# Norms of a layer's output tiles: sums taken with the residual's addition and squares on ScalarE, in place of statistics instructions

## The chip, the cores and the metric

The kernel runs on one core of one Trainium2 chip. Its engines are TensorE (PE for the products, PEld for loading their weights), VectorE (DVE), ScalarE (ACT), GpSimd (POOL) and SyncE (SP, which issues the transfers). Each engine has a queue of its own that it works through in order; an instruction that waits holds back all that stand behind it on that engine. The metric is the device time of one execution in microseconds.

## The reference

Four layers on x of 2048 rows by 640 columns, each `x = x + layer(layernorm(x))`: sliding-window attention, a Fourier mixing, attention again, Fourier mixing again.

```python
def _layernorm(x, axis=-1, eps=1e-5):
    m = jnp.mean(x, axis=axis, keepdims=True)
    v = jnp.var(x, axis=axis, keepdims=True)
    return (x - m) / jnp.sqrt(v + eps)
...
    x = A_x
    x = x + _A_ref(_layernorm(x, axis=-1), A_wqkv, A_wo)
    x = x + _B_ref(_layernorm(x, axis=-1), B_dft_seq_re, B_dft_seq_im, B_dft_hid_re, B_dft_hid_im)
    x = x + _A_ref(_layernorm(x, axis=-1), A_wqkv, A_wo)
    x = x + _B_ref(_layernorm(x, axis=-1), B_dft_seq_re, B_dft_seq_im, B_dft_hid_re, B_dft_hid_im)
    return x
```

`_A_ref` has 32 heads of width 20 with a window of 256, and ends in a product with `wo` (640 by 640). `_B_ref` is the real part of a Fourier transform over the hidden and the sequence dimension, written as products with matrices of cosines and sines.

## The kernel before

All large products are made in three parts: each operand is cut into a rounded piece (hi) and the rest (lo), and hi·hi + hi·lo + lo·hi is summed in PSUM. The cut is `split` (line 157): ACT writes hi (line 160), then DVE or, where `eng` says so, POOL subtracts to get lo (line 166).

The rows are worked on in 16 tiles of 128 (NB = 16). An attention layer ends in `after_heads`. By then the heads are done, and for each tile the product of the heads' outputs with the first three of five chunks of `wo` has been added to the residual; the sum lies in `y_part(t)`. What is left for each tile is in `late` (line 925): the product with the last two chunks (12 matrix products of 128x320, two halves in two PSUM banks in turn), the addition of each half to y into a tile xw (line 970; line 964 is the same for a tile made while heads still run), the store of xw, and the norm of xw, which the next layer needs.

The norm before takes `bn_stats` twice (line 218), `bn_aggr` (220), an addition of eps (222), a sign change of the mean (976), all on DVE; then the power -1/2 on POOL (`root`, line 981); then on ACT a one-column product (934) and the scaling of the whole tile (931), whose result goes back into `y_part(t)`. The next layer's first products use tiles in pairs j and j + 8. For t below 8, `split_x` cuts columns 0 to 384 of the normed tile (hi on ACT, lo on POOL). For t from 8 on, POOL first adds columns 384 to 640 of the pair's two tiles (`sum1`, line 1047), and `split_x` then cuts that sum. Tiles 14 and 15 (`fast`) go another way: DVE norms the columns that are needed first.

Between the tiles PE works on units of the Fourier layer (`unit`, `seq`; units 0 to 7 are "a1", unit 8 + j is "a2" of pair j): each multiplies one cut slice of a normed tile by one cut piece of the transform matrix, 9 products of 128x512. `cut_to` cuts these pieces one or two units ahead (the hi on ACT, sums and lo on DVE, line 166 with c or qp). When `let_go` is called, operations held back for the heads' outputs are written out (line 782, line 166 with kp).

The order of all this is written out once, by a planner in the program that counts time. `post(d, f)` writes f's instructions d ticks later; `tick` goes one tick on; `spend(us)` adds planned time and ticks once per 0.65 us (PACE). One step of a tile's product spends 0.147, a unit 2.05. A unit is written only when the tiles that it needs are normed and cut (`normed` against `need`); `after_heads` writes a tile, then one unit (two after tile 4), and so on. The posts of tile t, counted from the end of its additions: power +2; scaling +5; for t below 8 the cut +2 after that, for the others sum1 +1 and the cut +3 after that; the store of xw +5. `sum3` (line 1051, POOL) follows at +4 for t from 7 on.

The copies of line 1323 take finished sums of units 0 to 7 out of PSUM on ACT, posted +1, +4 and +7 after unit 7. ACT runs copies, scalings and, in the heads, exponentials.

Of the kernel before, what the change touches and what calls it, by code (L numbers as in the profile page):

```python
# [7 lines left out]
F32 = mybir.dt.float32  # L8
# [3 lines left out]
AF = mybir.ActivationFunctionType  # L12
OP = mybir.AluOpType
# [4 lines left out]
P = 128  # L18
S = 2048
D = 640  # L20
# [5 lines left out]
NB = S // P  # L26
# [3 lines left out]
EPS = 1e-5  # L30
# [33 lines left out]
class Net:  # L64
# [860 lines left out]
    def late(self, xsrc, xdst, hook):  # L925
        nc = self.nc
        ks = range(EARLY, KC)
        w = dict(zip(ks, self.late_w))

        def scaled(t, xw, st, nm, c0, c1):  # L930
            nc.scalar.activation(self.y_part(t)[:, c0:c1], xw[:, c0:c1], AF.Identity, bias=nm[:, 1:2], scale=st[1][:, 1:2])  # L931

        def norm(t, xw, st, nm):
            nc.scalar.activation(nm[:, 1:2], nm[:, 0:1], AF.Copy, scale=st[1][:, 1:2])
            scaled(t, xw, st, nm, 0, D)
            if t < NB // 2:
                self.post(2, lambda: self.split_x(t, 0, 384))
            else:
                j = t - NB // 2
                self.post(1, lambda: self.sum1(j, nc.gpsimd))  # L940
                self.post(3, lambda: self.split_x(j, 384, 640))

        def norm_last(t, xw, st):

            xn, j = self.y_part(t), t - NB // 2
            nc.vector.tensor_scalar(out=xn[:, 384:], in0=xw[:, 384:], scalar1=st[0][:, 0:1], scalar2=st[1][:, 1:2],
                                    op0=OP.subtract, op1=OP.mult)
            self.sum1(j, nc.vector)
            self.post(1, lambda: self.split_x(j, 384, 640, nc.vector))

        def norm_rest(t, xw, st, nm):
            nc.scalar.activation(nm[:, 1:2], nm[:, 0:1], AF.Copy, scale=st[1][:, 1:2])
            scaled(t, xw, st, nm, 0, 384)

        for t in range(NB):
            sb, i = t // 4, t % 4
            y = self.y_part(t)
            xw = self.raw()
            both = [slice(hf * 320, (hf + 1) * 320) for hf in range(2)]
            if not self.after:  # L960
                ps = [self.bank("w", 320) for _ in both]
                yield from self.in_turn(ps, [self.out_terms(self.late_o[sb], w, ks, i, hf) for hf in range(2)])
                for p, cs in zip(ps, both):
                    nc.vector.tensor_tensor(out=xw[:, cs], in0=p, in1=y[:, cs], op=OP.add)
            else:
                for hf, cs in enumerate(both):
                    p = self.bank("o", 320)
                    for _ in self.product3(p, self.out_terms(self.late_o[sb], w, ks, i, hf)):
                        yield 1
                    nc.vector.tensor_tensor(out=xw[:, cs], in0=p, in1=y[:, cs], op=OP.add)  # L970
                    if hf == 0:
                        yield 1
            self.post(5, lambda t=t, xw=xw: nc.sync.dma_start(xdst[t * P:(t + 1) * P, :], xw))
            st = self.stats(xw, False)
            nm = self.ln.tile([P, 2], F32, name="nb", tag="nb")
            nc.vector.tensor_scalar_mul(nm[:, 0:1], st[0][:, 0:1], -1.0)
            self.let_go()
            fast = t >= NB - 2

            def root(st=st):  # L980
                nc.gpsimd.tensor_tensor(out=st[1][:, 1:2], in0=st[1][:, 0:1], in1=self.half, op=OP.pow)  # L981
            if fast:
                root()
            else:
                self.post(2, root)
            if NB // 2 - 1 <= t < NB - 1:
                self.post(4, lambda t=t: self.sum3(t - NB // 2 + 1))
            if fast:
                d = 3 if t == NB - 2 else 0
                self.post(4 + d, lambda t=t, xw=xw, st=st: norm_last(t, xw, st))  # L990
                self.post(8 + d, lambda t=t, xw=xw, st=st, nm=nm: norm_rest(t, xw, st, nm))
            else:
                self.post(5, lambda t=t, xw=xw, st=st, nm=nm: norm(t, xw, st, nm))
            if t == NB - 2:
                u = self.last_a2 - 1
                self.post(3, lambda u=u: self.staged(u, 0, nc.vector))
                self.post(6, lambda u=u: self.staged(u, 1))
                self.post(9, lambda u=u: self.staged(u, 2))
            hook(t)
            self.late_t = t + 1  # L1000
            yield 0
# [728 lines left out]
```

## Time and profile before

| | us |
|---|---|
| median of 3 runs | 2174.63 (2174.54 to 2177.93) |
| the profiled execution, its own time | 2173.64 |
| its span from first to last instruction | 2171.9 |
| PE / DVE / ACT / POOL busy | 2116.4 / 1611.6 / 1167.9 / 932.6 |

The granted TensorE clock was 0.997 in the mean. A line of a profile names the source line, the engine, the operation, out<-in with their shapes and the count, then the busy time and the mean of one in ns, and after the second bar the engine's idle time just before such instructions, with what ended it. The chain of waits follows the work back from the last instruction, at each step to what released it, and lists the pieces in order of time: start, length, engine, tile, line. A table by stretches gives for each stretch the busy time of every engine, the granted clock, the share of the DMA engines and their GB/s. Rows of `big` hold the tiles y and their cut slices, `x` the tiles xw, `nb` the column that holds minus the mean, `rs` the one that holds the variance and its power, `c`, `qp`, `rr` cut pieces of the transform matrix.

The norms of the output tiles are made twice, at the end of layer 1 and of layer 3: 14 tiles the common way and two the fast way in each.

### The profile page before, as it was taken

What the parts mean: (1) busy time and instruction counts of PE and PEld (TensorE: products, weight loads), DVE (VectorE), ACT (ScalarE), POOL (GpSimd) and SP (SyncE); (2) the same over time, 40 slices, a digit from 0 to 9 for tenths busy, and PEclk for the clock granted to TensorE, in tenths of its full rate; (3) what the DMA queues carried; (4) which work ended last, traced back from release to release, by engine and by line L of the source; (5) the groups of instructions that cost most, each with busy time, mean ns of one, the idle gap of its engine ahead of it and who ended that gap; (6) DMA issues with size and microseconds to landing.
All of it is one profiled execution on the core that took longest, in us unless ns stands there. A gap on an engine that the chain in (4) does not pass through costs nothing.

```text
span 2171.9 us, 49261 instructions
## 1 busy us (share of the span) xinstructions
PE 2116.4 (97%) x17893; PEld 1768.5 (81%) x17893; DVE 1611.6 (74%) x3933; ACT 1167.9 (54%) x2611; POOL 932.6 (43%) x1458
## 2 busy tenths in 40 slices
PE   7999999899999999999999999998999999999999
PEld 7987777687878888889999877776777788888899
DVE  6348888786897968787751578887768878688777
ACT  3117887766554545543431288786665545455522
POOL 3037777876514224230230477777754333242300
PEclk9999999999999999999999999999999999999999
DMA  5546666786435353657646466667853454546653
GB/s 184 177 146 198 203 190 212 218 233 200 135 122 180 132 187 126 224 196 258 214 140 189 152 201 187 207 193 224 233 184 130 130 189 136 165 148 218 221 176 125
DMA packets 221619, 395.41 MB, mean 182 GB/s; under 512 B 39360, under 2 KB 85952, under 8 KB 221376
## 3 DMA queue, kind: packets, MB, share of 16 engines
q1 hardware_dynamic: 221376, 392.26, 57.0%
q8 instruction: 141, 2.31, 0.5%
q14 instruction: 102, 0.84, 0.1%
HBM read 273.94 MB, written 117.05 MB: 180 GB/s over the span
## 4 chain that ended last, share of the span: by engine, by line
PE 81%; DVE 6%; POOL 4%; ACT 4%; DMA 3%; issue 2%; SPq 0%; ACTq 0%; POOLq 0%; DVEq 0%
PE banks L1269 27%; PE banks L173 14%; PE banks L191 13%; PE banks L613 8%; PE banks L1524 6%; PE banks L583 6%; PE banks L553 4%; POOL ou L1199 1%; POOL big L166 1%; DVE qp L166 1%; ACT big L931 1%; PE banks L273 1%; PE banks L565 1%; POOL rs L981 1%; ACT big L160 1%
## 5 line engine op out<-in xcount | busy, mean ns | idle before, releaser
L558 DVE CUSTOM_DVE_ANT_0 banks<-banks,mask 128x384 f32<-128x384 f32 (+2 forms) x1024 | 525.5, 559 | 153.4 <-PE banks L553 117.5
L592 ACT ACTIVATE pt<-banks 128x384 f32<-128x384 f32 (+2 forms) x1024 | 430.1, 472 | 139.8 <-PE banks L553 59.5
L583 PE MATMUL banks<-qp,kp 61*128 61x384 f32 (+2 forms) x1024 | 302.8, 365 | 9.7 <-DMA qp<-mt 7.7
L598 POOL TENSOR_SCALAR_AFFINE_SELECT pt<-pt 128x256 f32<-128x256 f32 x512 | 213.5, 418 | 174.9 <-ACT pt L592 128.4
L553 PE MATMUL banks<-kp,qp 60*128 60x384 f32 (+2 forms) x1024 | 279.1, 359 | 4.8 <-DVE mc L558 4.5
L191 PE MATMUL banks<-big,wc 64*128 64x512 f32 x1920 | 272.1, 394 | 0.4 <-DVE pt L374 0.4
L583 PEld LDWEIGHTS banks<-qp,kp 61*128 61x128 f32 x1024 | 176.8, 185 | 68.0 <-issue 27.4
L613 PE MATMUL banks<-pt,vq 128*32 128x128 f32 x5760 | 215.3, 277 | 4.4 <-POOL pt L598 4.4
L191 PEld LDWEIGHTS banks<-big,wc 64*128 64x128 f32 x1920 | 183.3, 185 | 29.1 <-ACT x L477 6.7
L613 PEld LDWEIGHTS banks<-pt,vq 128*32 128x32 f32 x5760 | 144.3, 109 | 65.2 <-issue 48.2
L1199 POOL TENSOR_TENSOR pt<-pt,pt 128x512 f32<-128x512 f32 x36 | 62.8, 1744 | 293.0 <-DMA pt<-c 188.3
L602 POOL TENSOR_SCALAR_AFFINE_SELECT pt<-pt 128x256 f32<-128x256 f32 x448 | 187.4, 418 | 0.0
L553 PEld LDWEIGHTS banks<-kp,qp 60*128 60x128 f32 x1024 | 163.7, 185 | 26.7 <-DVE mc L558 16.3
L160 ACT ACTIVATE c<-pt 128x512 fp32r<-128x512 f32 x150 | 93.5, 626 | 151.0 <-POOL pt L1175 52.4
L160 ACT ACTIVATE qp<-pt 128x512 fp32r<-128x512 f32 (+1 forms) x195 | 119.9, 624 | 92.2 <-DVE pt L1200 38.9
L166 DVE TENSOR_TENSOR c<-pt,c 128x512 fp32r<-128x512 f32 x150 | 125.0, 843 | 52.0 <-ACT c L160 49.8
L166 DVE TENSOR_TENSOR qp<-pt,qp 128x512 fp32r<-128x512 f32 (+1 forms) x195 | 150.2, 783 | 12.4 <-ACT qp L160 9.8
L1269 PE MATMUL banks<-qp,big 128*128 128x512 f32 x630 | 151.2, 391 | 4.9 <-DVE qp L166 3.9
L558 DVE DVE_READ_ACCUMULATOR2_ANT mc<- 128x1 f32 x1024 | 145.2, 142 | 0.0
L1269 PEld LDWEIGHTS banks<-qp,big 128*128 128x128 f32 x630 | 117.0, 188 | 31.0 <-DVE qp L166 5.6
L1269 PE MATMUL banks<-qp,xc 128*128 128x512 f32 x480 | 117.9, 390 | 1.5 <-DVE xc L166 1.2
L1269 PEld LDWEIGHTS banks<-qp,xc 128*128 128x128 f32 x480 | 89.8, 188 | 21.9 <-DVE xc L166 2.1
(224 smaller groups left out, 4388.6 us busy)
## 6 DMA issues: line engine op xcount, KB each, us to landing
pt<-c SPq DMA_DIRECT2D x188, 512.0 KB
qk_d<-c SPq DMA_DIRECT2D x80, 512.0 KB
kp<-qk_d SPq DMA_DIRECT2D x384, 80.0 KB
qp<-qk_d SPq DMA_DIRECT2D x384, 80.0 KB
kp<-u_d SPq DMA_DIRECT2D x32, 640.0 KB
o_d<-ou SPq DMA_DIRECT2D x64, 256.0 KB
x_d<-x SPq DMA_DIRECT2D x48, 320.0 KB
v_d<-pt SPq DMA_DIRECT2D x16, 768.0 KB
```

What stands on the lines that cost most here:

```text
L160: nc.scalar.activation(hi, src, AF.Copy, scale=-1.0 if neg else 1.0)
L166: (eng or nc.vector).tensor_tensor(out=lo, in0=src, in1=hi.bitcast(F32), op=OP.subtract)
L173: self.nc.tensor.matmul(p, x, y, start=n == 0, stop=n == last)
L191: self.nc.tensor.matmul(ps[a], x[r], y[r], start=half + i == 0, stop=half == 1 and i == n - 1, skip_group_check=True)
L553: nc.tensor.matmul(p, qp[quad % 2][b:b + 60, z, qb * P:(qb + 1) * P], kp[quad % 2][b:b + 60, z, k0 * P:(qb + 1) * P], start=True, stop=True)
L558: nc.vector.tensor_tensor_reduce(out=p, in0=p, in1=self.mask[:, 384 - n * P:], scale=1.0, scalar=NEG, op0=OP.add, op1=OP.max, accum_out=mc ...
L583: nc.tensor.matmul(self.banks[:, tb[e], :n * P], kp[quad % 2][b:b + 61, z, kb * P:(kb + 1) * P], qp[quad % 2][b:b + 61, z, kb * P:(kb + n) ...
L592: nc.scalar.activation(pt[quad, kb][:, 2 * z + e, :n * P], self.banks[:, tb[e], :n * P], AF.Exp, scale=SCALE)
L598: nc.gpsimd.affine_select(out=t[:, :, 0:P], in_=t[:, :, 0:P], pattern=[[0, 2], [1, P]], compare_op=OP.is_ge, fill=0.0, base=0, channel_mul ...
L602: nc.gpsimd.affine_select(out=t[:, :, 256:384], in_=t[:, :, 256:384], pattern=[[0, 2], [-1, P]], compare_op=OP.is_gt, fill=0.0, base=0, ch ...
L613: nc.tensor.matmul(p[32 * h:32 * h + 32, :], vq[:, 96 * (kb % 4) + 21 * h:96 * (kb % 4) + 21 * h + 32], t[:, h, (qb - kb) * P:(qb - kb + 1 ...
L1269: nc.tensor.matmul(self.banks[:, bk, :], p, b[q], start=start and m == 0, stop=stop and last and m == 2, skip_group_check=True)
```

## The change

For tiles 0 to 13, the additions of line 970 become additions that also give each row's sum (`tensor_tensor_reduce`, the instruction that the heads use at line 558 with a maximum), into a new small tile `sa`. One DVE operation makes minus the mean of the two sums. The square of xw minus the mean is written by ACT (into y, where it is overwritten later by the scaling) with its row sum, one DVE operation makes the variance plus eps from it, and the power follows on POOL as before. `bn_stats`, `bn_aggr`, the addition of eps and the sign change go, for these tiles. The posts become: square +1, variance +3, power +4 (was +2), scaling +6 (was +5); what hangs on the scaling moves with it. Tiles 14 and 15 keep the instructions that they had.

```diff
+            fast = t >= NB - 2
+            sa = None if fast else self.ln.tile([P, 3], F32, name="sa", tag="sa")
+
+            def add(p, hf, y=y, xw=xw, sa=sa):
+                cs = both[hf]
+                if sa is None:
+                    nc.vector.tensor_tensor(out=xw[:, cs], in0=p, in1=y[:, cs], op=OP.add)
+                else:
+                    nc.vector.tensor_tensor_reduce(
+                        out=xw[:, cs], in0=p, in1=y[:, cs], scale=1.0, scalar=0.0,
+                        op0=OP.add, op1=OP.add, accum_out=sa[:, hf:hf + 1])
...
-                    nc.vector.tensor_tensor(out=xw[:, cs], in0=p, in1=y[:, cs], op=OP.add)
+                    add(p, hf)
...
-            st = self.stats(xw, False)
             nm = self.ln.tile([P, 2], F32, name="nb", tag="nb")
-            nc.vector.tensor_scalar_mul(nm[:, 0:1], st[0][:, 0:1], -1.0)
+            if fast:
+                st = self.stats(xw, False)
+                nc.vector.tensor_scalar_mul(nm[:, 0:1], st[0][:, 0:1], -1.0)
+            else:
+                st = None, self.ln.tile([P, 2], F32, name="rs", tag="rs")
+                nc.vector.tensor_scalar(out=nm[:, 0:1], in0=sa[:, 0:1], scalar1=sa[:, 1:2], scalar2=-1.0 / D,
+                                        op0=OP.add, op1=OP.mult)
             self.let_go()
-            fast = t >= NB - 2
...
+            def square(xw=xw, y=y, nm=nm, sa=sa):
+                nc.scalar.activation(y, xw, AF.Square, bias=nm[:, 0:1], scale=1.0, accum_out=sa[:, 2:3])
+
+            def variance(st=st, sa=sa):
+                nc.vector.tensor_scalar(out=st[1][:, 0:1], in0=sa[:, 2:3], scalar1=1.0 / D, scalar2=EPS,
+                                        op0=OP.mult, op1=OP.add)
             if fast:
                 root()
             else:
-                self.post(2, root)
+                self.post(1, square)
+                self.post(3, variance)
+                self.post(4, root)
...
             else:
-                self.post(5, lambda t=t, xw=xw, st=st, nm=nm: norm(t, xw, st, nm))
+                self.post(6, lambda t=t, xw=xw, st=st, nm=nm: norm(t, xw, st, nm))
```

More of the change, by code (lines that the diff above doesn't have):

```diff
@@ L962, in late @@
                 yield from self.in_turn(ps, [self.out_terms(self.late_o[sb], w, ks, i, hf) for hf in range(2)])
-                for p, cs in zip(ps, both):
-                    nc.vector.tensor_tensor(out=xw[:, cs], in0=p, in1=y[:, cs], op=OP.add)
+                for hf, p in enumerate(ps):
+                    add(p, hf)
             else:
@@ L969, in late @@
                         yield 1
-                    nc.vector.tensor_tensor(out=xw[:, cs], in0=p, in1=y[:, cs], op=OP.add)
+                    add(p, hf)
                     if hf == 0:
```

## The prediction

> **What bounds the kernel now.** I read the page's first part and chain of waits, then the stage that the change touches, by its line 970 (durations shortest/median/longest, then first and last start).
>
> ```profile
> span 2171.9 us, 49261 instructions
> PE 2116.4 (97%) x17893; PEld 1768.5 (81%) x17893; DVE 1611.6 (74%) x3933; ACT 1167.9 (54%) x2611; POOL 932.6 (43%) x1458
> PE 81%; DVE 6%; POOL 4%; ACT 4%; DMA 3%; issue 2%; SPq 0%; ACTq 0%; POOLq 0%; DVEq 0%
> ```
>
> ```profile
> L970 DVE TENSOR_TENSOR x<-banks,big x64: 473/478/492, 525.6 to 1666.0; 128x320 f32<-128x320 f32 x64
> ```
>
> TensorE sets the end of the whole, so only what moves TensorE counts. The table by stretches (columns: length, then busy us of PE, PEld, DVE, ACT, POOL) shows the stage of layer 1 in two parts and the second part of layer 3:
>
> ```profile
> 525.00:545.00 20.00, 16.58 (x92) 14.03 (x92) 19.23 (x49) 11.58 (x21) 8.48 (x10) 1.00 0.69 227
> 545.00:592.62 47.62, 44.62 (x235) 38.43 (x233) 40.23 (x104) 25.21 (x50) 27.07 (x34) 1.00 0.44 145
> 1625.00:1672.36 47.36, 44.32 (x234) 38.16 (x232) 39.96 (x104) 25.20 (x50) 27.07 (x34) 1.00 0.45 146
> ```
>
> The two layers agree, so I work out one stage and double it. PE is idle 3.42 + 3.00 = 6.4 us per stage: that is all that the change could win there. DVE is full in the first 20 us (19.23); ACT and POOL look half empty. They are not free, though. The chain of waits through the stage, in order of time (start, length, what):
>
> ```profile
> 548.07 0.93 ACT big L931
> ...
> 557.94 0.93 ACT big L931
> 558.87 0.52 ACT c L160
> 559.39 0.43 ACT big L160
> ...
> 559.88 1.53 POOL big L166
> 561.41 0.96 POOL rs L981
> ...
> 562.73 0.93 ACT big L931
> ...
> 566.66 0.92 ACT big L931
> 567.59 0.52 ACT qp L160
> 568.10 0.36 ACT kp L1323
> ...
> 568.49 0.41 ACT big L160
> ...
> 568.97 0.74 POOL big L166
> 569.71 0.52 POOL rs L981
> 570.25 0.30 ACT nb L934
> ...
> 570.58 0.92 ACT big L931
> ...
> 582.26 0.92 ACT big L931
> 583.18 0.53 ACT c L160
> ...
> 592.62 0.50 PE banks L1269
> ```
>
> This is the row to learn from. From tile 5 (548.07) to tile 13 (582.26) the chain never touches PE. It is a ring through two queues that each run in order: ACT scales tile t (L931), cuts a transform piece (L160 into c or qp), rounds tile t's slice (L160 into big); POOL takes the rounding's rest (L166), and only behind that, in its queue, the power for tile t+1 (L981); ACT's next scaling waits for that power. One turn in the second half is 566.66 to 570.58, 3.92 us, and PE's own turn, from tile to tile, is hardly shorter, 3.82:
>
> ```profile
> 566.45 1.92 PE L173 MATMUL banks<-qp,kp 128*128 128x320 f32 x12
> ...
> 570.27 1.92 PE L173 MATMUL banks<-qp,kp 128*128 128x320 f32 x12
> ```
>
> After tile 13 the chain goes on in one line through a piece for DVE, the last addition and the fast path of tile 15, to the last product at 592.62. So what is added to each turn of the ring reaches the end of the stage.
>
> **The change part by part.** The prices:
>
> ```profile
> L218 DVE BATCH_NORM_STATS2 st<-x 128x6 f32<-128x320 f32 x32 | 14.0, 477 | 0.0
> L220 DVE BATCH_NORM_AGGREGATE mv<-st 128x2 f32<-128x12 f32 x16 | 3.3, 209 | 0.5
> L976 DVE TENSOR_SCALAR nb<-mv 128x1 f32<-128x1 f32 x16 | 2.3, 144 | 0.0
> L558 DVE CUSTOM_DVE_ANT_0 banks<-banks,mask 128x384 f32<-128x384 f32 x896 | 482.1, 584 | 117.7 <-PE banks L553 99.6 <-PE banks L583 3.8
> L558 DVE DVE_READ_ACCUMULATOR2_ANT mc<- 128x1 f32 x1024 | 145.2, 142 | 0.0
> L233 ACT ACTIVATE kp<-kp,nm 128x640 f32<-128x640 f32 x9 | 7.4, 824 | 15.0 <-POOL nm L232 15.0
> ```
>
> *Removed on DVE*, per tile 0 to 13: two statistics 2 x 0.477, the aggregate 0.21, and two one-column operations of 0.14 (L976's row): 1.44 us.
>
> *Added on DVE.* The addition with a sum is the operation of L558, which in this kernel always brings a read of the accumulator. Its 0.584 is for 384 columns; for 320 it lies between the plain addition's 0.478 and that, and I take 0.53; the read is 0.142. Twice: 2 x (0.53 + 0.14 - 0.48) = 0.38. Two one-column operations (the mean, the variance) 0.29. So DVE gains 1.44 - 0.67 = 0.77 us per tile, 11 us per stage. Where DVE is what PE waits for, that could be time. Two such places are beyond the first tiles:
>
> ```profile
> 540.53 2.14 PE L1269 MATMUL banks<-qp,big 128*128 128x512 f32 x8 [1.23 <-DVE qp L166]
> 554.87 2.03 PE L173 MATMUL banks<-qp,kp 128*128 128x320 f32 x12 [0.75 <-DVE x L970]
> ```
>
> *Added on ACT.* A square of 128x640 with a column bias. The trace has no square and no ACT sum. The nearest row is L233, the same shape with a column bias: 0.824; back to back it gives way about 0.09 early (the scaling of 566.66 lasts 0.92 and is followed by the row below), so 0.74 is the lower end, as if the sum were free. The upper end is L931's step of 0.83 and another one-column step on ACT (nb at 570.25 to the scaling at 570.58: 0.33): 1.16. I take 0.93, near the middle, since DVE's sum costs a read of its own.
>
> ```profile
> 567.49 0.61 ACT L160 ACTIVATE qp<-pt 128x512 fp32r<-128x512 f32 x1
> ```
>
> *Moved.* Posts count ticks of 0.65 us of planned time; a tile (12 steps of 0.147) and a unit (2.05) make 3.81 us, 5.87 ticks. Relative to tile t's own post, before: power +2, scaling +5, rounding +7 (tiles below 8) or +8. After: square +1, variance +3, power +4, scaling +6, rounding +8 or +9. The square of tile t+1 thus comes at +6.9: in ACT's queue behind the scaling of tile t (+6) and ahead of its rounding (+8 or +9). POOL's order is kept: rounding's rest of tile t, then the power of tile t+1 (+9.9). So the square is put *into* the ring, once per turn. The order of PE's work stays: working the ticks through, units 0 and 1 still come after tile 4 (unit 1 needs tile 2 rounded by its check at tick 16; it is, at 15), and later checks have ticks to spare. The store of the tile stays at +5 on SP, and tile buffers (five in turn) are held a few us longer of some 19 us, so neither costs.
>
> *The sum to tile 13.* Tile 5: its power now waits for a variance that stands in DVE's queue behind what `let_go` puts there, two products of line 782:
>
> ```profile
> 546.61 0.69 DVE L782 TENSOR_TENSOR pt<-pt,vq 128x512 f32<-128x512 f32 x1
> ```
>
> That is 0 to 1.4 us, taken 0.8 (the square and the power's own wait run beside it). Turns 5 to 8 (three): between scaling and rounding there is no gap (558.87 to 559.39 follow on each other), so the whole square counts, 0.74 to 1.16 each, taken 0.93: 2.8. Against it, POOL's 1.53 and 0.96 at 559.88 are twice its 0.74 and 0.52 of 568.97; if that is DVE's doing, a lighter DVE gives back 0 to 1.6 over the three; taken 0.75. Turns 8 to 13 (five): ACT reaches the rounding 1.83 us after the scaling (566.66 to 568.49) of which its own work is 0.83 + 0.52 = 1.35, so 0.48 of the square hides behind POOL's sum (L1047): 0.26 to 0.68 left, taken 0.45: 2.25. The copies of L1323 (568.10) hid in the same gap; two of the three now stand ahead of a rounding: 0 to 1.0, taken 1.0. Together 0.8 + 2.8 - 0.75 + 2.25 + 1.0 = 6.1 us per stage; all low ends 0 + 2.2 - 1.6 + 1.3 + 0 = 1.9, all high ends 1.4 + 3.5 + 3.4 + 1.0 = 9.3.
>
> *What gives way, and what waits next.* Behind the chain's last link PE has no slack: the products of the slice of tile 13 start as its rest is done. DVE's gains in the first 20 us and at 554.87 do not reach the end, because the ring, not PE, is last from 548 on. A new wait appears: the variance on DVE waits for ACT's square, and behind it on DVE stand the next tile's additions, for which PE's next tile waits (two banks in turn). It holds PE back at the pace of the ring, and adds nothing as long as the ring is slower anyway. Tiles 14 and 15 are unchanged.
>
> So 2 x 6.1 = 12.2 us on the profiled execution's own 2173.64 us: 2185.8. The median of the runs is 1.0 us above that execution; I say **2186**.
>
> **The rivals.**
>
> *A: DVE's relief wins (faster).* If squares fell into ACT's waits, the ring would keep its 3.9 us. For it:
>
> ```profile
> ACT nb L934 <- POOL rs L981: 22.6, 13, 5.0
> ```
>
> ACT waits 22.6 us for powers in a stage, and 14 squares are 13 us. Then the waits on DVE go: PE's whole idle time of the first 20 us, 3.42, and the 0.75 at 554.87, 4.2 per stage, of which I would count 3; 2174.6 - 6 = 2168.6. It decides if ACT's queue had the square behind the rounding, in the 1.4 us in which it waits for POOL; the ticks say otherwise. 12%.
>
> *B: no difference.* The low ends of the sum together with some of A's gains: 1.9 less 1 to 2 per stage, 2174.6 within 0.2%. It needs a free sum on ACT, and POOL's long operations to shrink. 14%.
>
> *C: DVE held up harder.* If the variance, waiting for the square, makes the next tile's additions the last thing in each turn, a turn grows by these as well: 2 x 0.48 over some eight turns, 7.7 us more per stage, 2201. Against it: from square to square that way is only square, variance, two additions and mean, some 2.3 us, well below the ring's turn. 8%.
>
> *D: table loads.*
>
> ```profile
> L160 ACT ACT_TABLE_LOAD x1 | 1.3, 1283 | 0.8 <-PEq L1720 0.8
> ```
>
> One load serves the whole program now. If the square sits in another set than copy and scaling, each of 28 squares brings two loads: 28 x 2 x 1.28 = 72 us in the ring, about 2255. If one change at each end of a stage does, four loads, mostly in ACT's idle time before the first scaling. I give the first 2%, and the second lies within the range. The Trainium skill, page "ScalarE: Activation LUTs", section "Table sets: the hidden batching unit", says that copy and identity are in every set as filler; by that rule only the second case is left, and 2186 stands. No run here shows it yet.
>
> **How the numbers follow.** My forecast (slower through the ring) has 64%, its own range 2178 to 2193 by the ends of its sum; A 12%, B 14%, C 8%, D 2%. A measurement of this kernel tells about 0.2% (4.4 us) from no change. Slower: the forecast, C and D, 74%; within 0.2%: B, 14%; faster: A, 12%. The range 2174 to 2194 takes in the forecast's, and half of B; it leaves out A, most of C, and D.
>
> **What would show it.** Right: in the chain of waits of the changed kernel a square stands between L931 and the rounding in each turn; turns of 4.3 to 4.6 us in the second half; tile 13's scaling some 6 us later after the first addition than now (582.26 less 525.6, 56.7 us); DVE idle on the square ahead of the variance; PE waiting for the additions near tiles 12 to 15. Wrong: the turns stay at 3.9 us, or the rounding runs ahead of the square in ACT's queue, or PE's units come in another order; DVE's busy time of the stage not falling by some 10 us; table loads at the squares.

## The result, and the profile after

The changed kernel is slower: 2180.72 us (2178.01 to 2187.92, 9 runs) against 2174.54 (2171.97 to 2177.93, 9 runs) for the kernel before; the ratio is 1.0033, with a 95% interval of 1.0024 to 1.0042, or 5 to 9 us.

The first part of the page of the changed kernel, with the order of its lines as before:

```profile
span 2178.1 us, 49255 instructions
PE 2117.4 (97%) x17893; PEld 1765.7 (81%) x17893; DVE 1579.7 (73%) x3905; ACT 1189.1 (55%) x2667; POOL 925.5 (42%) x1458
```

DVE does 32 us less in the whole (1611.6 to 1579.7) and ACT 21 us more, as the edit means it to be; PE's busy time stays and the span grows. (Some 5 of the 32 us are spread between executions: two of the experiments below keep the statistics, and their DVE was busy for 1606.4 and 1607.3 us.) The table by stretches shows where DVE's relief is (length, then busy us of PE, PEld, DVE, ACT, POOL, the granted clock, the DMA engines' share and GB/s):

```profile
525.00:545.00 20.00, 16.80 (x93) 14.30 (x92) 15.48 (x46) 16.05 (x33) 9.21 (x10) 1.00 0.70 238
545.00:592.62 47.62, 42.61 (x219) 35.16 (x217) 27.70 (x85) 28.91 (x60) 25.31 (x34) 1.00 0.37 124
```

In the second stretch DVE falls from 40.23 to 27.70, and yet PE does less in the same time, 42.61 where it did 44.62. The chain of waits of the changed kernel shows why (start, length, what; L1000 is the square with the read of its sum, L997 the power, L1294 the units' products):

```profile
547.50 0.93 ACT big L931
...
558.29 0.92 ACT big L931
559.22 0.81 ACT big L1000 x2
560.03 0.52 ACT c L160
560.55 0.42 ACT big L160
...
561.04 1.09 POOL big L166
562.13 0.52 POOL rs L997
562.67 0.30 ACT nb L934
...
563.00 0.92 ACT big L931
...
567.43 0.92 ACT big L931
568.35 0.52 ACT qp L160
568.88 0.81 ACT big L1000 x2
569.69 0.48 ACT kp L1348
570.17 0.32 ACT big L160
...
570.55 0.74 POOL big L166
571.29 0.52 POOL rs L997
571.84 0.30 ACT nb L934
...
572.16 0.92 ACT big L931
...
585.36 0.92 ACT big L931
586.28 0.53 ACT c L160
...
595.73 10.47 PE banks L1294 x43
```

It is the ring of before with one link more: between a tile's scaling and its rounding stands the next tile's square, 0.81 us. The turn that was 3.92 us (566.66 to 570.58) is 4.73 (567.43 to 572.16); over the five turns from tile 8 to 13 the mean is 4.47 against 3.91, since part of the square falls into time in which ACT waited for POOL's sum of two tiles (1.4 us of such waits in this stage before, 0.3 after). From tile 13's scaling to the last link it is 595.73 - 585.36 = 10.37 us, as before (592.62 - 582.26 = 10.36): nothing is gained or lost behind the ring.

Since the two executions reach the stage at different times, lengths are counted from the start of the first addition of an output tile. Of the changed kernel, these are the first addition on DVE and, from the list of waits in the stage (who waited for whom: us in total, times, longest), what PE and DVE wait for:

```profile
524.16 0.49 DVE L968 CUSTOM_DVE_ANT_0 x<-banks,big 128x320 f32<-128x320 f32 x1 [0.39 <-PE banks L173]
```

```profile
PE banks L173 <- DVE sa L968: 5.3, 6, 1.5
...
DVE rs L1003 <- ACT big L1000: 2.5, 4, 1.2
```

The stage is 595.73 - 524.16 = 71.57 us in layer 1 and 71.54 in layer 3; before it was 592.62 - 525.62 = 67.00 and 67.01. That is 4.55 us per stage, 9.1 in all. The span grew by 6.2 only, because the one profiled execution of before took 1012.7 us from the end of its first stage to the first addition of the second, where the profiles of the changed kernel and of all the experiments took 1009.1 to 1011.7, and also began its first stage 1.5 us later than that of the changed kernel (525.62 and 524.16). The ratio of the runs, 5 to 9 us, holds the 9.1 at its upper end. The clock may have a part in the median as well: the profiled run and one more have a mean granted clock of 0.997 and took 2179.8 and 2178.0 us, the other seven have 0.993 to 0.995 and took 2180.2 to 2187.9; what lowered it in those is not shown.

### The profile page after: what moved, and what is told of

Same layout as the page of the kernel before. It is cut to its first block, busy times and chain, and to the rows that moved or that the text cites. A ratio compares the mean times of both kernels' runs of the same rounds, so it can differ in the third digit from the quotient of the medians.

```text
span 2178.1 us, 49255 instructions
## 1 busy us (share of the span) xinstructions
PE 2117.4 (97%) x17893; PEld 1765.7 (81%) x17893; DVE 1579.7 (73%) x3905; ACT 1189.1 (55%) x2667; POOL 925.5 (42%) x1458
## 4 chain that ended last, share of the span: by engine, by line
PE 81%; DVE 6%; ACT 5%; POOL 4%; DMA 2%; issue 2%; SPq 0%; ACTq 0%; DVEq 0%; POOLq 0%
PE banks L1294 27%; PE banks L173 14%; PE banks L191 14%; PE banks L613 8%; PE banks L1549 6%; PE banks L583 6%; PE banks L553 4%; POOL ou L1224 1%; POOL big L166 1%; ACT big L1000 1%; DVE qp L166 1%; ACT big L931 1%; ACT big L160 1%; ACT qp L160 1%; PE banks L273 1%
## 5 line engine op out<-in xcount | busy, mean ns | idle before, releaser
L598 POOL TENSOR_SCALAR_AFFINE_SELECT pt<-pt 128x256 f32<-128x256 f32 x512 | 210.7, 412 | 177.9 <-ACT pt L592 131.5
L602 POOL TENSOR_SCALAR_AFFINE_SELECT pt<-pt 128x256 f32<-128x256 f32 x448 | 184.6, 412 | 0.0
L160 ACT ACTIVATE c<-pt 128x512 fp32r<-128x512 f32 x150 | 93.6, 626 | 145.1 <-POOL pt L1200 51.8
L160 ACT ACTIVATE qp<-pt 128x512 fp32r<-128x512 f32 (+1 forms) x195 | 119.9, 624 | 90.8 <-DVE pt L1225 37.6
L166 DVE TENSOR_TENSOR qp<-pt,qp 128x512 fp32r<-128x512 f32 (+1 forms) x195 | 150.1, 783 | 23.2 <-ACT qp L160 20.4
L166 DVE TENSOR_TENSOR c<-pt,c 128x512 fp32r<-128x512 f32 x150 | 121.5, 820 | 60.4 <-ACT c L160 58.5
L1294 PE MATMUL banks<-qp,big 128*128 128x512 f32 x630 | 151.6, 391 | 6.2 <-DVE qp L166 3.9
L1294 PEld LDWEIGHTS banks<-qp,big 128*128 128x128 f32 x630 | 117.0, 188 | 32.8 <-DVE qp L166 5.4
L1294 PE MATMUL banks<-qp,xc 128*128 128x512 f32 x480 | 117.9, 390 | 1.6 <-DVE xc L166 1.4
L1294 PEld LDWEIGHTS banks<-qp,xc 128*128 128x128 f32 x480 | 89.8, 188 | 22.1 <-DVE xc L166 2.2
```

Source lines behind the costliest of these rows:

```text
L160: nc.scalar.activation(hi, src, AF.Copy, scale=-1.0 if neg else 1.0)
L166: (eng or nc.vector).tensor_tensor(out=lo, in0=src, in1=hi.bitcast(F32), op=OP.subtract)
L598: nc.gpsimd.affine_select(out=t[:, :, 0:P], in_=t[:, :, 0:P], pattern=[[0, 2], [1, P]], compare_op=OP.is_ge, fill=0.0, base=0, channel_mul ...
L602: nc.gpsimd.affine_select(out=t[:, :, 256:384], in_=t[:, :, 256:384], pattern=[[0, 2], [-1, P]], compare_op=OP.is_gt, fill=0.0, base=0, ch ...
L1294: nc.tensor.matmul(self.banks[:, bk, :], p, b[q], start=start and m == 0, stop=stop and last and m == 2, skip_group_check=True)
```

## The experiments

Each experiment's stage is measured in the same way, from the starts of the scalings (L931) of tiles 5, 8 and 13, counted from the first addition, and of the product at the end of the chain; all values are us, of layer 3, from one profiled execution of each kernel. The times are medians, with the ratio to the kernel before, which ran again beside the experiments (2173.4 us beside the first four of them, 2174.1 beside the last four).

| kernel | tile 5 | tile 8 | tile 13 | turn, tiles 8 to 13 | stage | time | ratio (95%) |
|---|---|---|---|---|---|---|---|
| before | 22.46 | 37.12 | 56.65 | 3.91 | 67.01 | 2174.5 | |
| changed | 23.32 | 38.81 | 61.17 | 4.47 | 71.54 | 2180.7 | 1.0033 (1.0024 to 1.0042) |
| changed, variance and power at +1 | 23.75 | 35.64 | 53.49 | 3.57 | 65.08 | 2169.0 | 0.9978 (0.9968 to 0.9987) |
| before, power at +1 | 22.39 | 35.62 | 53.58 | 3.59 | 64.71 | 2169.1 | 0.9981 (0.9972 to 0.9991) |
| changed, square twice in place | 28.02 | 46.78 | 73.92 | 5.43 | 84.29 | 2207.1 | 1.0155 (1.0139 to 1.0170) |
| changed, second square later | 25.41 | 40.89 | 63.27 | 4.48 | 74.34 | 2188.5 | 1.0075 (1.0060 to 1.0090) |
| before, later posts | 22.46 | 37.12 | 56.69 | 3.91 | 67.15 | 2173.8 | 0.9998 (0.9989 to 1.0008) |
| changed, square of one column | 21.89 | 36.46 | 56.56 | 4.02 | 67.09 | 2171.7 | 0.9984 (0.9975 to 0.9994) |
| changed, variance on POOL | 23.36 | 40.27 | 64.69 | 4.88 | 75.06 | 2188.5 | 1.0060 (1.0044 to 1.0076) |
| mixture, power at +1 | 24.34 | 37.47 | 54.51 | 3.41 | 65.65 | 2170.1 | 0.9979 (0.9969 to 0.9988) |

In some of these executions the granted clock fell to half for 3.4 us at a time. In layer 3, with the square twice in place and with the variance on POOL, such a stretch lies in the chain just ahead of tile 5: seven products of PE's unit there take 0.43 us each in place of 0.23, some 1.4 us in all. The turns of the closed ring touch no PE, so the other stretches do not lengthen them.

**Opening the ring in the changed kernel.** The one link that need not be there is POOL's: the power of tile t+1 has nothing to do with the rest of tile t, and only stands behind it in the queue.

```diff
                 self.post(1, square)
-                self.post(3, variance)
-                self.post(4, root)
+                self.post(1, variance)
+                self.post(1, root)
```

> The changed kernel with variance and power posted +1 (right behind the square) in place of +3 and +4, so that POOL's queue has the power of tile t+1 ahead of the rounding's rest of tile t. Stage length below is from the first addition of an output tile to the start of the product at the end of the chain (before 67.0 us in both layers, after 71.6 and 71.5). Theory of the ring: the ring loses POOL's rest (0.74); a turn is then ACT's own work alone, 0.83 scaling + 0.52 piece + 0.81 square + 0.42 rounding + 0.33 column = 2.9 us, less than PE's 3.82. Turns from tile 8 to 13 fall from 4.47 to 3.8 or 3.9, the stage to 64.5 to 66.5, the time to 2169 to 2173. Rival (what costs is that DVE waits for ACT's squares, or ACT's work as such): the squares and the wait are still there, the wait even earlier in DVE's queue: stage 71 to 72, time about 2181.

The turn fell to 3.57 us and the stage to 65.08, by 6.5 us, with every square still in place, and the wait of DVE for it longer than in the changed kernel (there 2.5 us in 4 waits):

```profile
DVE rs L1003 <- ACT big L1000: 7.6, 8, 1.7
```

The chain of waits of this kernel is PE alone from unit 1 to tile 14:

```profile
541.52 2.11 PE banks L1294 x8
543.62 1.75 PE banks L173 x12
545.38 2.06 PE banks L1294 x9
...
576.14 2.06 PE banks L1294 x9
578.20 1.77 PE banks L173 x12
```

The rival, in which the squares cost as ACT's work or through DVE's wait, falls. The turn came out below the 3.82 us that was expected as a floor, since the scalings, late after the first 20 us, catch up with PE.

**Opening it in the kernel before.** If the ring set that kernel too, the same edit must help it.

```diff
-                self.post(2, root)
+                self.post(1, root)
```

> The kernel before with the power posted +1 in place of +2, so that it stands ahead of the rounding's rest in POOL's queue; nothing else is changed. Theory of the ring: the ring set the kernel before too, at 3.91 us a turn against PE's 3.82; opened, turns from tile 8 to 13 come to 3.82, tile 13's scaling comes earlier by 1 to 2 us and the stage shrinks from 67.0 to 65.5 to 66.8, time 2170 to 2174. Rival (PE and DVE set the stage before, the ring only kept pace): 67.0 and 2174.5.

It did: the stage fell to 64.71 us and the time to 2169.1, so the ring was a bound already, not only a chain that kept pace. POOL's queue in this kernel shows the order, the power (L981) ahead of the rest (L166):

```profile
563.11 0.74 POOL L1047 TENSOR_TENSOR big<-big,big 128x256 f32<-128x256 f32 x1
563.81 1.00 POOL L981 TENSOR_TENSOR rs<-rs,half 128x1 f32<-128x1 f32 x1
564.78 0.74 POOL L166 TENSOR_TENSOR big<-big,big 128x256 fp32r<-128x256 f32 x1
```

The gain, 2.3 us per stage, was larger than expected (0.2 to 1.5). With the ring open the two ways of making the norm differ by 0.4 us per stage, in favour of the statistics, and their times cannot be told apart: DVE's relief buys nothing there either.

**A second square, in the ring and out of it.** Both kernels do the same added work on ACT, 14 squares per stage; only its place differs.

```diff
             def square(xw=xw, y=y, nm=nm, sa=sa):
-                nc.scalar.activation(y, xw, AF.Square, bias=nm[:, 0:1], scale=1.0, accum_out=sa[:, 2:3])
+                for _ in range(2):
+                    nc.scalar.activation(y, xw, AF.Square, bias=nm[:, 0:1], scale=1.0, accum_out=sa[:, 2:3])
```

> The changed kernel with every square computed twice, one right behind the other (the same result written again). Theory of the ring: each turn grows by one more square, 0.81; over the turns from tile 5 to 13 the stage grows by 5.5 to 7, to 77 to 79 us, time about 2193. The rival that looks at ACT's busy time expects the same here; it parts from the ring in the run where the second square stands elsewhere.

```diff
+            def again():
+                nc.scalar.activation(xw, xw, AF.Square, bias=nm[:, 0:1], scale=1.0, accum_out=sa[:, 2:3])
...
-                self.post(2, lambda: self.split_x(t, 0, 384))
+                self.post(2, lambda: (self.split_x(t, 0, 384), again()))
...
-                self.post(3, lambda: self.split_x(j, 384, 640))
+                self.post(3, lambda: (self.split_x(j, 384, 640), again()))
```

> The changed kernel with a second square per tile as well, but written right behind the rounding of that tile, where ACT waits for POOL (1.4 to 1.5 us a turn); it goes into the tile xw, which is stored and normed by then, and its sum is not used. Theory of the ring: the work falls into the wait and costs nothing: stage 71 to 73 us, time 2179 to 2184. Rival (ACT's added work as such): as with the square computed twice in place, 77 to 79 us and about 2193.

The turns answer as a ring does: in place, a second square makes each turn from tile 8 to 13 0.96 us longer (5.43 against 4.47); behind the rounding it makes it 0.01 longer (4.48). Both stages came out longer than expected, 84.29 us for 77 to 79 and 74.34 for 71 to 73, and so did the times (2207.1 for about 2193, 2188.5 for 2179 to 2184). In place, 8.05 of the 12.75 us more lie in the eight turns from tile 5 on, for which 5.5 to 7 was expected, and 4.7 ahead of tile 5, some 1.4 of them with the stretch at half clock. Behind the rounding, 2.1 of the 2.8 us lie ahead of tile 5 and 0.7 behind the ring. In the first 20 us ACT is busy for 16.05 in the changed kernel, and in both of these kernels four second squares stand in the chain of waits there; behind tile 13, one more stands in the chain ahead of a piece (ACT x L935, 0.91 us, before c L160). So the second place is free in the turns, but not in the stage as a whole. That a turn grew by 0.96 and not by 0.81 is seen on ACT in the kernel with the square in place twice: the second square, which writes the same y and the same sum, starts only after the read of the first's sum has ended, 0.94 after the first.

```profile
578.42 0.82 ACT L1001 ACTIVATE big<-x,nb 128x640 f32<-128x640 f32 x1
579.14 0.18 ACT L1001 ACTIVATION_READ_ACCUMULATOR big<-x,nb 128x1 f32 x1
579.36 0.83 ACT L1001 ACTIVATE big<-x,nb 128x640 f32<-128x640 f32 x1
```

**The later posts alone.** The kernel before, with the power and the scaling posted as late as in the changed one.

```diff
-                self.post(2, root)
+                self.post(4, root)
...
-                self.post(5, lambda t=t, xw=xw, st=st, nm=nm: norm(t, xw, st, nm))
+                self.post(6, lambda t=t, xw=xw, st=st, nm=nm: norm(t, xw, st, nm))
```

> The kernel before with only the change's later posts: power +4 in place of +2, scaling +6 in place of +5; statistics and additions as before. Theory of the ring: POOL's and ACT's queues keep the order that closes the ring and nothing is added to it, so 3.9 us a turn and a stage of 66.8 to 67.4, time 2174. Rival (the later posts are what costs, 0.65 us of planned time each): the scalings come 0.65 to 1.3 us later per turn or once, stage 68 to 71.

No difference: 67.15 us, turns of 3.91, ratio 0.9998. (The profiled execution was the longest of the ten, 2179.3 us; its excess lies ahead of the first stage, which began at 532.22.) Later ticks cost nothing here, where the order in each queue stays.

**The square cut down to one column.** All instructions, waits and posts of the change, without the square's length.

```diff
-                nc.scalar.activation(y, xw, AF.Square, bias=nm[:, 0:1], scale=1.0, accum_out=sa[:, 2:3])
+                nc.scalar.activation(y[:, 0:1], xw[:, 0:1], AF.Square, bias=nm[:, 0:1], scale=1.0, accum_out=sa[:, 2:3])
```

> The changed kernel with the square taken of one column in place of 640, so the variance is left out; all instructions, waits and posts stay. Theory of the ring: the square's step falls from 0.81 to some 0.3 us, which hides behind POOL's sum of two tiles; turns from tile 8 to 13 fall from 4.47 to 3.9 or 4.0 and the stage to 65.5 to 67.5, time 2171 to 2175: DVE's lighter load by itself buys nearly nothing with the ring closed. Rivals: if the new waits and later posts cost, and not the square's length, it stays at 71; if DVE's load set the stage before, it falls to 63 or 64.

The stage came back to 67.09 us (66.68 in layer 1), turns 4.02. So all of the 4.5 us go with the square's length. This kernel has DVE's relief in full, 12 to 15 us per stage (1581.9 us busy in all, against 1606.4 to 1611.6 with the statistics), and its stage is no shorter than that of before: tile 5 comes 0.57 earlier, and the five turns, with the short square still in the ring, take 0.57 more. The time, at 0.9984, is 1 to 5 us below that of before, more than the stages show. Whether that is the spread of the parts outside them, a microsecond or two between executions, or a gain of the change there, is not shown.

**DVE freed of the wait.** The variance moved to POOL, ahead of the power.

```diff
-                nc.vector.tensor_scalar(out=st[1][:, 0:1], in0=sa[:, 2:3], scalar1=1.0 / D, scalar2=EPS,
+                nc.gpsimd.tensor_scalar(out=st[1][:, 0:1], in0=sa[:, 2:3], scalar1=1.0 / D, scalar2=EPS,
...
-                self.post(3, variance)
+                self.post(4, variance)
```

> The changed kernel with the variance computed on POOL, right ahead of the power, in place of DVE, so that DVE never waits for a square of ACT. Theory of the ring: the ring gets one more POOL instruction per turn (a one-column one took 0.2 to 0.75 us in the scaling of line 232), turns of 4.6 to 5.0 and a stage of 72.5 to 76, time 2182 to 2190, though PE's waits on DVE's additions change their releaser. Rival (what costs is DVE held up by the wait for the square): the stage falls to 68 or less, time 2175 or less.

DVE no longer waits for a square, and the stage grew by 3.5 us to 75.06. All of it lies in the eight turns (1.4 in those from tile 5 to 8, 2.0 in those from 8 to 13), whose chain has one link of POOL more, the variance. In this kernel's list of waits PE still waits for the additions, though DVE waits for no square; together with the opened ring, where DVE waits longer and the stage is shorter, this shows that PE's wait follows the ring and does not set it:

```profile
PE banks L173 <- DVE sa L968: 6.2, 6, 1.4
```

**A mixture.** With the ring open, the change's way for tiles 1, 3 and 5 to 10, the statistics for the others.

```diff
+            plain = fast or t in (0, 2, 4, 11, 12, 13)
...
-                self.post(6, lambda t=t, xw=xw, st=st, nm=nm: norm(t, xw, st, nm))
+                self.post(5, lambda t=t, xw=xw, st=st, nm=nm: norm(t, xw, st, nm))
```

(In it, the `if fast` of the statistics is `if plain`, and square and variance are posted only for the others.)

> A version meant to be the fastest: power +1 for all tiles (ring open), scaling +5, sums and squares for tiles 1, 3 and 5 to 10 with the variance at +1, the statistics of before for tiles 0, 2, 4 and 11 to 13. Theory: with the ring open, the first 15 us are set by ACT where all tiles have squares and by DVE where none has, so a mixture is shorter than either: stage 63.8 to 64.8 us (64.7 with statistics alone, 65.1 with squares alone), time 2166 to 2169. Rival (the first part is set by PE and the transfers): 64.7 to 65.1.

It missed: 65.65 us in layer 3 (in layer 1 the granted clock was 0.83 for 10 us of the stage, so its 66.74 is not used), later at tile 5 than either pure kernel. What sets the first 15 us in a mixture was not followed further. The times of the three kernels with the power at +1 (2169.0, 2169.1, 2170.1) cannot be told apart; by the stage the shortest is the kernel before with that post.

## Why the prediction was right

The direction, the mechanism and the place were right, and the size was too large: 2186 was forecast from two stages of 6.1 us more each; a stage measured 4.55, and the time came out at 2180.7.

- *The order in the queues.* Working out the ticks gave a square between a tile's scaling and its rounding, and the power still behind the rest. The chain of waits shows both. PE's units came in the same order.
- *The square's price.* Taken 0.93, between 0.74 and 1.16; measured 0.81 a step (0.818 and a read of 0.187, which overlap).
- *Tile 5.* Taken 0.8 later, measured 0.86 to 0.89. That the number fits is in part luck, since its parts were others. Between the additions and the end of the variance lie some 3.5 us (542.96 to 546.52), for two products of L782 (0.67 and 0.97 us of the chain) and two more operations of DVE (0.68 and 0.60), where 0 to 1.4 had been allowed; against this the statistics of before (1.4 us) are gone, the additions come 0.9 earlier, and POOL's power takes 0.56 in place of 1.02.
- *Turns 5 to 8: the term that was mis-sized.* Three squares less what a lighter DVE gives back on POOL: taken 2.8 - 0.75 = 2.05, measured 0.84 (15.50 against 14.66). The squares are 3 x 0.81 = 2.4, and 1.6 came back, the very upper bound: 1.3 on POOL itself (powers 2.92 to 2.01 us, rests 3.58 to 3.16, by the chain) and 0.25 because tile 7's power no longer waits for DVE's statistics. POOL's powers in these turns and a rest, before:

```profile
552.02 1.00 POOL L981 TENSOR_TENSOR rs<-rs,half 128x1 f32<-128x1 f32 x1
...
556.59 0.99 POOL L981 TENSOR_TENSOR rs<-rs,half 128x1 f32<-128x1 f32 x1 [0.25 <-DVE nb L976]
...
559.88 1.53 POOL L166 TENSOR_TENSOR big<-big,big 128x384 fp32r<-128x384 f32 x1 [1.50 <-ACT big L160]
561.37 1.00 POOL L981 TENSOR_TENSOR rs<-rs,half 128x1 f32<-128x1 f32 x1
```

and after:

```profile
552.31 0.54 POOL L997 TENSOR_TENSOR rs<-rs,half 128x1 f32<-128x1 f32 x1
...
556.94 1.00 POOL L997 TENSOR_TENSOR rs<-rs,half 128x1 f32<-128x1 f32 x1
...
561.04 1.09 POOL L166 TENSOR_TENSOR big<-big,big 128x384 fp32r<-128x384 f32 x1 [2.40 <-ACT big L160]
562.09 0.54 POOL L997 TENSOR_TENSOR rs<-rs,half 128x1 f32<-128x1 f32 x1
```

  The same instruction on a single column takes 1.00 or 0.54 us, and which of the two goes with what DVE is doing. The power at 556.94 starts while DVE subtracts one piece of an SBUF tile from another:

```profile
556.80 0.72 DVE L1200 TENSOR_TENSOR pt<-pt 128x512 f32<-128x512 f32 x1
```

  Those at 552.31 and 562.09 start beside additions from PSUM and one-column operations. Over the whole trace of before, all 18 powers that start during a DVE operation on two SBUF tiles take 0.99 to 1.13 us, and in the changed kernel all 12 (0.99 to 1.14); the others take 0.54 to 0.57, or 0.78 to 0.85 where DVE scales a tile (L236). The Trainium skill, page "SBUF — State Buffer", section "🔬 SBUF: two separate sides", says that a VectorE operation with two SBUF inputs and a GpSimd operation that reads SBUF shut each other out of a shared pair of ports, each for a whole instruction. The powers of 1.00 and 0.54 us agree with that; no run here took DVE's work away alone at this place.
- *Turns 8 to 13.* Taken 2.25 + 1.0 = 3.25, measured 2.83 (22.36 against 19.53), with the two copies of L1323 (L1348 in the changed kernel) in the way as expected.
- *Behind the ring.* No slack was assumed from tile 13 to the last link: 10.37 against 10.36 us.
- *DVE's relief.* Taken 11 us per stage; DVE's busy time fell by 31.9 in all between the two profiled executions, 16 for each of the two stages. Of that the instructions that the change swaps account for 12.9, more than 11 because the read of a sum takes 0.083 us here and not 0.142, and the addition 0.485 and not 0.53; the rest are other operations of DVE that ran shorter, and spread. It bought nothing in the stage, as forecast; the square of one column shows it.
- *The rivals.* A's condition was the right one: a square behind the rounding costs a turn 0.01 us, though 2.8 us per stage outside the turns. C, DVE held up by the wait, is refuted by the opened ring and by the variance on POOL. For D, one table load serves the changed kernel as it did the one before, so square, copy, scaling and exponential work from one set.

What the prediction did not draw from its own chain is that the ring bound the kernel before, and that a post of +1 for the power would open it.

## What to carry to other kernels

Half-empty engines can still be the bound: here the chain of waits went round through two in-order queues and did not touch the busy engine from tile 5 on. What is put between two links of such a ring is paid on every turn, less what falls into a wait that is already between them (the square's 0.81 us cost 0.57 a turn from tile 8 to 13, with the copies that it pushed into the chain; a second one cost 0.96); what is put into the wait beside the links is free in the turns (0.01 us), though not where the ring has not yet begun or has ended. Look for the link that is there only by its place in a queue, and move that one first: one tick of one post made the stage of the kernel before 2.3 us shorter. Relief on an engine that such a ring passes by buys nothing; here it bought nothing when the ring was open, either, since PE then set the pace.

## What had not been expected of the hardware

ACT's sum is a separate instruction, a read of 0.187 us that overlaps the operation before it by about 0.1; a second square into the same tile and sum waits for its end (0.94 from start to start instead of 0.81). DVE's read of a sum took 0.142 us behind the heads' maximum and 0.083 here. A power of one column on POOL took 0.54 us, and 1.00 where it started during a DVE operation on two SBUF tiles. The granted clock fell to half for 3.4 us at a time in the stages of five of the eight experiments, and in none of those of the two profiled executions of before and after; with the square twice in place there were three such stretches in each stage. What sets them off was not followed.
